# First pair's queries and keys read in fp32 by SyncE's queue and converted on chip, pair 0's bias rows fetched by SyncE's queue: the opening of a fused attention and feed-forward kernel

## The chip, the cores and the metric

The kernel runs on one core of one Trainium2 chip. The metric is the device time of one execution in microseconds (us). Each profile is one such execution, and times inside it count from the span's start. PE is TensorE, ACT ScalarE, DVE VectorE, POOL GpSimd, SP SyncE. All runs used here are of the fast state, except e8's single run, whose state can't be told. Runs of the same kernel still differ by 1.7 us (changed kernel, 17 runs) to 2.9 us (kernel before, 39 runs), which matters for everything below.

## The reference, cut to what matters

```python
# q, k, v: (8, 8, 576, 64) fp32; bias_table: (32, 8)
scores = q @ k.transpose(0, 1, 3, 2) / 8 + bias[bucket]      # relative-position bias per head
attn   = softmax(scores)
x      = (attn @ v)  -> (4608, 512)
out    = ((x @ w_a) * (x @ w_b)) @ w_out                      # bilinear feed-forward
```

Heads are worked on in 32 pairs; "pair 0" is the first two heads of the first batch. The bias is applied after the exponential, as a multiplication by exp(bias), whose rows lie in a small table that the kernel computes and writes to DRAM.

## The kernel before: the parts concerned

Almost all inputs are cast to bf16 on their way by POOL's loads. An "opening" string gives the hand-made order of the first 70 us or so: `<k0` is a load, `TK0`/`TQ0` transposes of pair 0's keys and queries on PE, `CK`/`CQ` copies of them out of PSUM (`:A` on ACT, `:D` on DVE), `S001` a score block (pair, half, key block), `E001` its exponential on ACT, `M001` the multiplication by bias on DVE, `w1` a filler: a multiplication of zeros on PE.

```python
def load4(src, dst, b, h0, h1):                       # casts fp32 -> bf16, POOL
    nc.gpsimd.dma_start(
        out=dst[:, 256 * h0:256 * h1].rearrange("p (h x) -> p h x", x=256),
        in_=src[b, h0:h1, 0:SM, :].rearrange("h (p t) d -> p h (t d)", t=NM))
# ...
nc.sync.dma_start(out=bt_sb[0:NB, :], in_=bias_table)
nc.scalar.dma_start(out=bl_sb[0:NB, :], ...)
nc.sync.dma_start(out=oh_sb[0:NB, :], in_=oh_handle.ap())     # one-hot buckets
nc.scalar.dma_start(out=ident[:, :], in_=id_handle.ap())      # identity for transposes
# ...
warm_up(5)
nc.scalar.activation(out=eb_sb[0:NB, :], in_=bt_sb[0:NB, :], func=ACTF.Exp)
nc.tensor.matmul(out=tps[0:H, 0:NR], lhsT=eb_sb[0:NB, :], rhs=oh_sb[0:NB, :], ...)
warm_up(2)
# ...
nc.sync.dma_start(out=tab.ap(), in_=tab_sb[0:H, :])           # the bias table, to DRAM

def load_w(hp, y0, y1):                               # bias rows of a pair, POOL
    nc.gpsimd.dma_start(out=W_sb[hp][:, :, y0:y1], in_=bass.AP(tensor=tab, ...))
# ...
opening = """
    <k0 <q0 <k1 <q123h0 <k23 <tk <W0 <v0 <W1 <vtb <vta ...
    <wb2 <wo TK0 PC0:A TQ0 PF1:D PX1:D PV1:A PU0:D CK0:A CQ00:A CQ01... w1 S001 ... S000 E001 E000
    w1 TQ30 PC1:D TK1 ... TQ10 CQ10:D S011 E011 ...                      # cut
"""
```

The softmax here doesn't subtract the row's maximum and nothing guards it: scores larger than these inputs give would overflow.

## Time and profile before

| | kernel before |
|---|---|
| median of 3 runs (first measurement) | 414.23 us |
| PE busy | 404.5 of 412.2 us |
| first exponential on ACT | 8.01 us |
| pair 0's keys and queries landed | 4.4 (first used at 4.70) and 6.15 us |
| bias table landed (POOL goes on) | 8.31 us |
| PE at full clock from | 13.9 us |

The timeline of PE around 13.9 us (columns: start, length, engine, line, operation, result and operands, shape, count).

```profile
13.35 0.61 PE L446 MATMUL qkh<-QT,KT 64*128 64x256 bf16 x4
13.88 0.39 PE L237 MATMUL warm<-zero_sb 128*128 128x512 bf16 x1
14.21 0.39 PE L446 MATMUL qkh<-QT,KT 64*128 64x256 bf16 x4
```

The same four score multiplications take 0.61 us ahead of 13.88 us and 0.39 us after it. That is how to read the release of PE's clock from a profile: the clock row of the page shows 9 in all slices and the table of windows 1.00 even before 13.9 us, since the trace's clock record only begins with its first change, here at 13.86 us.

### The profile page before, as it was taken

What the parts mean: (1) busy time and instruction counts of PE and PEld (TensorE: products, weight loads), DVE (VectorE), ACT (ScalarE), POOL (GpSimd) and SP (SyncE); (2) the same over time, 40 slices, a digit from 0 to 9 for tenths busy, and PEclk for the clock granted to TensorE, in tenths of its full rate; (3) what the DMA queues carried; (4) which work ended last, traced back from release to release, by engine and by line L of the source; (5) the groups of instructions that cost most, each with busy time, mean ns of one, the idle gap of its engine ahead of it and who ended that gap; (6) DMA issues with size and microseconds to landing.
All of it is one profiled execution on the core that took longest, in us unless ns stands there. A gap on an engine that the chain in (4) does not pass through costs nothing.

```text
span 412.2 us, 8768 instructions
## 1 busy us (share of the span) xinstructions
PE 404.5 (98%) x3473; PEld 210.0 (51%) x3473; DVE 240.8 (58%) x568; ACT 251.3 (61%) x384; POOL 133.6 (32%) x191
## 2 busy tenths in 40 slices
PE   8999999999999999999999999999999999999996
PEld 3576656455555455455444555555545554444443
DVE  3898997366745665476656764667547652421320
ACT  4998992676748665677556765767486642322321
POOL 6967547788029300960079004300000000000000
PEclk9999999999999999999999999999999999999999
DMA  8999999999979914995299709960520012002004
GB/s 104 179 202 189 206 166 144 160 193 142 87 133 159 139 34 91 155 129 90 41 161 143 116 16 126 127 92 17 117 67 16 17 40 78 0 9 95 2 2 102
DMA packets 135786, 42.05 MB, mean 102 GB/s; under 512 B 113688, under 2 KB 130968, under 8 KB 135744
## 3 DMA queue, kind: packets, MB, share of 16 engines
q0 software_dynamic: 81712, 20.27, 56.3%
q1 hardware_dynamic: 48592, 11.87, 18.6%
q10 hardware_dynamic: 5440, 9.34, 7.2%
q8 instruction: 27, 0.44, 0.5%
q14 instruction: 15, 0.12, 0.1%
HBM read 39.18 MB, written 9.45 MB: 118 GB/s over the span
## 4 chain that ended last, share of the span: by engine, by line
PE 94%; DVE 2%; ACT 2%; DMA 1%; issue 1%; ACTq 0%; POOL 0%; POOLq 0%
PE pb L633 23%; PE pa L633 23%; PE po L670 22%; PE av L569 8%; PE qk L406 7%; PE av L559 2%; PE av L563 2%; PE qkh L446 1%; PE qkt L479 1%; DMA qn<-in_q_dram 1%; PE trb L321 1%; ACT ath L452 1%; PE trb L415 1%; PE trb L609 0%; DVE ath L461 0%
## 5 line engine op out<-in xcount | busy, mean ns | idle before, releaser
L430 ACT ACTIVATE at<-qk 128x1024 bf16<-128x1024 f32 x112 | 113.3, 1028 | 27.5 <-DMA out_dram<-ob 10.3
L643 DVE TENSOR_TENSOR g<-pb,ha 128x512 bf16<-128x512 f32 (+1 forms) x114 | 75.6, 664 | 75.0 <-PE pb L633 58.9
L633 PE MATMUL pb<-xn,wb 128*128 128x512 bf16 (+1 forms) x456 | 112.1, 368 | 0.2 <-DVE g L643 0.2
L633 PE MATMUL pa<-xn,wa 128*128 128x512 bf16 (+1 forms) x456 | 112.1, 368 | 0.0
L640 ACT ACTIVATE ha<-pa 128x512 f32<-128x512 f32 (+1 forms) x114 | 66.2, 581 | 67.7 <-PE pa L633 66.2
L670 PE MATMUL po<-wo,g 128*128 128x512 bf16 x420 | 98.2, 379 | 0.0
L435 DVE TENSOR_TENSOR at<-at,W 128x1024 bf16<-128x1024 bf16 x112 | 75.1, 686 | 22.2 <-ACT at L430 22.1
L633 PEld LDWEIGHTS <-wa 128*128 128x128 bf16 x456 | 41.2, 98 | 46.3 <-issue 6.6
L633 PEld LDWEIGHTS <-wb 128*128 128x128 bf16 x456 | 40.6, 97 | 43.6 <-issue 5.2
L670 PEld LDWEIGHTS <-g 128*128 128x128 bf16 x420 | 38.9, 98 | 44.9 <-issue 2.5
L675 ACT ACTIVATE ob<-po 128x512 f32<-128x512 f32 x34 | 20.4, 600 | 39.9 <-PE po L670 33.6
L569 PE MATMUL av<-vm,at 128*128 128x65 bf16 x896 | 41.2, 193 | 0.0
L569 PEld LDWEIGHTS <-at 128*128 128x128 bf16 x896 | 37.4, 97 | 6.3
L132 POOL DMA_DIRECT2D qn<-in_q_dram x48 | 36.4, 807 | 12.0 <-PE qk L406 6.9
L170 POOL DMA_DIRECT2D vt<-in_v_dram x12 | 7.4, 620 | 98.9 <-PE av L563 98.1
L580 DVE RECIPROCAL rc<-av 128x6 f32<-128x6 f32 (+1 forms) x64 | 11.9, 186 | 45.2 <-PE av L569 40.8
L141 POOL DMA_DIRECT2D kn<-in_k_dram x48 | 36.2, 794 | 1.4 <-issue 0.7
L559 PE MATMUL av<-vt,att 128*128 128x130 bf16 x152 | 33.6, 221 | 0.0
L406 PE MATMUL qk<-QB,KB 64*128 64x512 bf16 x192 | 29.1, 381 | 0.0
L582 DVE TENSOR_TENSOR XG<-av,rc 128x384 bf16<-128x384 f32 (+2 forms) x64 | 27.2, 425 | 2.2
L506 ACT ACTIVATE att<-qkt 128x640 bf16<-128x640 f32 x24 | 16.8, 701 | 13.0 <-PE qkt L480 13.0
L559 PEld LDWEIGHTS <-att 128*128 128x128 bf16 x152 | 15.0, 98 | 6.5
(104 smaller groups left out, 327.0 us busy)
## 6 DMA issues: line engine op xcount, KB each, us to landing
out_dram<-ob ACTq DMA_DIRECT2D x31, 256.0 KB, 3.1
vn<-in_v_dram POOLq DMA_DIRECT2D x16, 256.0 KB, 5.8
kn<-in_k_dram POOLq DMA_DIRECT2D x48, 64.0 KB, 5.0
qn<-in_q_dram POOLq DMA_DIRECT2D x48, 64.0 KB, 4.4
wa<-in_moe_w_a_dram POOLq DMA_DIRECT2D x3, 512.0 KB, 7.4
wb<-in_moe_w_b_dram POOLq DMA_DIRECT2D x3, 512.0 KB, 9.2
wo<-in_moe_w_out_dram POOLq DMA_DIRECT2D x1, 1536.0 KB, 15.6
xn<-XG SPq DMA_TRANSPOSE x52, 3.0
```

The lines of the kernel that those rows point to most:

```text
L132: nc.gpsimd.dma_start(out=by_tile(qn[b % 2])[:, h0 // 4, t, :, :], in_=q[b, h0:h1, 128 * t:128 * t + 128, :].transpose([1, 0, 2]))
L141: nc.gpsimd.dma_start(out=by_tile(kn[b % 2])[:, h0 // 4, t, :, :], in_=k[b, h0:h1, t:SM:NM, :].transpose([1, 0, 2]))
L406: nc.tensor.matmul(out=ps[:, hh, :], lhsT=kT[r, t, :], rhs=qT[r, :, :], start=True, stop=True)
L430: nc.scalar.activation(out=at[:, :, :], in_=ps[:, :, :], func=ACTF.Exp, scale=scale)
L435: nc.vector.tensor_tensor(out=at[:, :, :], in0=at[:, :, :], in1=w[:, :, S - 1 + t:S - 1 + t - SM:-1], op=MULT)
L559: nc.tensor.matmul(out=pav[:, slot, :, :], lhsT=weights_tail(p, jq), rhs=vt[i][:, :, hp, :], start=True, stop=True)
L569: nc.tensor.matmul(out=pav[:, slot, hh, :], lhsT=weights(p, t, hh, jq), rhs=vm[i][:, 2 * hp + hh, t, :], start=False, stop=True, skip_grou ...
L582: nc.vector.tensor_tensor(out=xg[:, jqs[0]:jqs[0] + m, :, :], in0=pav[:, 0:m, :, 0:Dh], in1=rc[:, 0:m, :].unsqueeze(3).to_broadcast([128, ...
L633: nc.tensor.matmul(out=ps[:, 0:n], lhsT=w[df // 4][:, mc, 128 * (df % 4):128 * (df % 4) + 128], rhs=xn_sb[mc][:, 512 * c + lo:512 * c + lo ...
L640: nc.scalar.activation(out=ha[:, 0:n], in_=ff["pa", df, lo][:, 0:n], func=ACTF.Copy)
L643: nc.vector.tensor_tensor(out=g_sb[df][:, lo:lo + n], in0=ff["pb", df, lo][:, 0:n], in1=ff["ha", df, lo][:, 0:n], op=MULT)
L670: nc.tensor.matmul(out=po[:, :], lhsT=g_sb[df][:, 128 * tt:128 * tt + 128], rhs=wo_sb[:, df, :], start=(df == 0), stop=(df == NDF - 1))
```

## The change

Its intent: SyncE's queue is idle at the start while POOL's list of casting loads is long. So pair 0's queries and keys are read as fp32 by SyncE and converted by ACT and DVE, POOL starts with other loads, and pair 0's bias rows also go to SyncE, right behind the table's store. The two constants become one load, and the opening is put in a new order.

```diff
-    nc.sync.dma_start(out=bt_sb[0:NB, :], in_=bias_table)
+    def load_first(x, dst):
+        nc.sync.dma_start(out=dst.rearrange("p (h x) -> p h x", x=256),
+                          in_=x[0, 0:2, 0:SM, :].rearrange("h (p t) d -> p h (t d)", t=NM))
+    nc.sync.dma_start(out=cn_sb[:, :], in_=cn_handle.ap())     # identity and one-hot, joined
+    load_first(q, kq32[1])
+    load_first(k, kq32[0])
+    nc.scalar.dma_start(out=bt_sb[0:NB, :], in_=bias_table)
 ...
-            load_w(int(name[1]), *(...))
+            load_w(int(name[1]), *(...), nc.sync if name in ('W0',) else nc.gpsimd)
 ...
-        <k0 <q0 <k1 <q123h0 <k23 <tk <W0 <v0 <W1 <vtb <vta <tq <W2 <R0 ...
-        <wb2 <wo TK0 PC0:A TQ0 ... w1 S001 PX0:D CQ01:A S000 E001 E000
-        w1 TQ30 PC1:D TK1 CK1:D TQ10 CQ10:D S011 E011 ...
+        <q123h0 <k1 <tk <vtb <k23 <W1 <W0 <v0 <vta <tq <W2 <W3 ...
+        PC0:A PX0:D YQ0:A PC1:A PU0:D PV0:A PX1:D TQ0 YK0:D TK0 CQ00:A CQ01:D CK0:D TQ10 PF1:A CQ10:D
+        S000 E000 PV1:D S001 E001 TK1 CK1:D TQ30 TZ1 CZ1:D S011 ...
 ...
+        elif kind == "YK":
+            copy(eng, kn[0][:, 0:512], kq32[0])                 # fp32 -> bf16
+        elif kind == "YQ":
+            copy(eng, qn[0][:, 0:512], kq32[1])
```

More of the change, by code (lines that the diff above doesn't have):

```diff
@@ L73 @@
     oh_np[bucket, np.arange(NR)] = 1.0
-    oh_handle = nc.inline_tensor(oh_np.astype(ml_dtypes.bfloat16), name="oh_const")
-    id_handle = nc.inline_tensor(np.eye(128).astype(ml_dtypes.bfloat16), name="id_const")
-    oh_sb = const.tile([128, NR], BF16, name="oh_sb")
-    ident = const.tile([128, 128], BF16, name="ident")
+    cn_np = np.zeros((128, NR + 128), dtype=np.float32)
+    cn_np[0:NB, 0:NR] = oh_np
+    cn_np[:, NR:] = np.eye(128)
+    cn_handle = nc.inline_tensor(cn_np.astype(ml_dtypes.bfloat16), name="cn_const")
+    cn_sb = const.tile([128, NR + 128], BF16, name="cn_sb")
+    oh_sb = cn_sb[:, 0:NR]
+    ident = cn_sb[:, NR:NR + 128]
     bt_sb = const.tile([128, H], FP32, name="bt_sb")
@@ L114 @@
     ob_last = wpool.tile([128, DM], FP32, name="ob_last")
+    kq32 = [xn_sb[i][:, NT - 1024:NT].bitcast(FP32) for i in range(2)]
     g_sb = [wpool.tile([128, DM], BF16, name=f"g{df}") for df in range(NDF)]
@@ L224 @@
                                     ap=[[0, NB], [1, H]]))
-    nc.sync.dma_start(out=oh_sb[0:NB, :], in_=oh_handle.ap())
-    nc.scalar.dma_start(out=ident[:, :], in_=id_handle.ap())
     nc.vector.memset(zero_sb[:, :], 0.0)
@@ L249, with load_w @@
     nc.vector.tensor_copy(out=tab_sb[0:H, c0:c0 + NR], in_=tps[0:H, 0:NR])
-    def load_w(hp, y0, y1):
-        nc.gpsimd.dma_start(out=W_sb[hp][:, :, y0:y1],
+    def load_w(hp, y0, y1, eng):
+        eng.dma_start(out=W_sb[hp][:, :, y0:y1],
                           in_=bass.AP(tensor=tab, offset=2 * hp * TB + y0,
@@ L295, in load @@
         elif name[0] in "WR":
-            load_w(int(name[1]), *((320, NY) if name[0] == "W" else (0, 320)))
+            load_w(int(name[1]), *((320, NY) if name[0] == "W" else (0, 320)), nc.sync if name in ('W0',) else nc.gpsimd)
         else:
@@ L728 @@
     opening = """
-        <k0 <q0 <k1 <q123h0 <k23 <tk <W0 <v0 <W1 <vtb <vta <tq <W2 <R0 <v1 <Wta <q123h1 <W3 <Wtb <R1
-        <wa0 <k4 <wb0 <R2 <R3 <q4 <k5 <uq <q7 <q5 <wa1 <wb1 <k6 <uk <vt1b <k7 <vb1a <vb1b <vt1a <wa2 <q6
-        <wb2 <wo TK0 PC0:A TQ0 PF1:D PX1:D PV1:A PU0:D CK0:A CQ00:D w1 S001 PX0:D CQ01:A S000 E001 E000
-        w1 TQ30 PC1:D TK1 CK1:D TQ10 CQ10:D S011 E011 CQ30:D TK3 S100 E100 TZ1 CK3:D S301 M001 TQ20
-        PV0:D TK2 E301 S101 E101 CQ20:D CK2:D w1 S200 E200 CZ1:D M000 w1 KS w1 S201 EK w2 S010 E201 V0:D
@@ L734 @@
-        M101 TZ0 M100 M200 M201 AV00 N00 CZ0:A AV10 E010 X00 CX00:A S300 E300 N10 T0 V1:D X10 CX10:A
-        M010 ET0 AV20 TQ11 TQ21 M011 N20 CQ11:A S110 S111 CQ21:A E110 X20 M301 TQ31 M300 AV30 T1 PW:D
-        MT0 AV01 CX20:D M110 E111 N30 ET1 X30 M111 CQ31:A T2 ET2 S210 CX30:D E210 PF0:A LH FA0a N01 HA0a
-        MT1 TK4 X01 T3 AV11 ET3 CX01:D S211 PU1:D FB0a FA1a E211 CK4:D HA1a N11 X11 G0a M210 S310 MT2
-        CX11:A E310 FB1a G1a S311 FA2a HA2a TQ4 M211 CQ4:A FB2a AV21 E311 FA3a HA3a TQ5 MT3 M310 S43 S42
@@ L739 @@
-        CQ5:A G2a FB3a N21 M311 TK5 E43 E42 TZ0x G3a CZ0x:D AV31 LV CK5:D N31 FA4a HA4a X21 TQ7 CQ7:A
-        S41 E41 S52 E52 CX21:D FB4a FA5a HA5a X31 G4a TK6 M43 FB5a CX31:D S40 E40 S53 G5a FA0b FB0b
-        CK6:D M41 TZ1x HA0b G0b CZ1x:D S51 FA1b FB1b E53 M53 HA1b G1b E51 TK7 CK7:D M40 FA2b HA2b S50
-        E50 FB2b FA3b G2b HA3b V2:D T4 FB3b FA4b V3:D ET4 G3b S70 E70 M42 MT4 M52 HA4b FB4b G4b TQ6 T5
-        ET5 M50 CQ6:A AV40 N40 MT5 M51 FA5b S71 E71 HA5b S73 FB5b AV41 G5b M70 N41 S72 E73 FA6f E72 T6
@@ L744 @@
-        M73 M71 HA6f FB6f G6f AV50 N50 S62 ET6 MT6 E62 S61 FA7f HA7f M62 AV51 N51 TH S60 E61 M61 FB7f
-        G7f E60 M60 S63 E63 M63 FA8f HA8f M72 T7 FB8f G8f AV60 N60 ET7 MT7 FA9f HA9f FB9f G9f AV70 FA10f
-        FB10f N70 HA10f G10f AV71 FA11f N71 FB11f X71 HA11f G11f AV61 N61 X70 FO00 FO01 FO02 HO0 CX70:D
-        CX71:D
+        <q123h0 <k1 <tk <vtb <k23 <W1 <W0 <v0 <vta <tq <W2 <W3 <v1 <Wta <q123h1 <R0 <Wtb <R1 <k4 <wa0
+        <wb0 <R2 <uq <q5 <q4 <R3 <k5 <wa1 <q7 <wb1 <k6 <uk <k7 <vb1a <vb1b <vt1a <q6 <wb2 <vt1b <wa2 <wo
@@ new lines @@
+        PC0:A PX0:D YQ0:A PC1:A PU0:D PV0:A PX1:D TQ0 YK0:D TK0 CQ00:A CQ01:D CK0:D TQ10 PF1:A CQ10:D
+        S000 E000 PV1:D S001 E001 TK1 CK1:D TQ30 TZ1 CZ1:D S011 CQ30:D E011 S101 TQ20 CQ20:D E101 M101
+        S100 E100 TK3 CK3:D KS EK M000 TK2 S301 E301 CK2:D w2 S200 E200 M100 M001 w1 S201 E201 V0:D
+        PU1:D w2 S300 E300 M200 M201 AV00 TZ0 AV10 S010 CZ0:A N00 T0 N10 E010 X10 X00 CX00:A V1:D AV20
+        CX10:A TQ11 TQ21 M301 M300 ET0 AV30 CQ11:A S110 CQ21:A N20 M010 M011 PW:A MT0 S111 TQ31 E110 X20
@@ new lines @@
+        CQ31:A E111 T1 ET1 N30 M110 X30 CX20:D CX30:D AV01 T2 TK4 M111 S210 ET2 E210 FA0a HA0a N01 T3
+        MT1 X01 AV11 CK4:D CX01:A PF0:D LH ET3 N11 S211 E211 FB0a FA1a HA1a X11 G0a MT2 CX11:D S310 E310
+        FB1a G1a S311 M210 FA2a FB2a HA2a E311 TQ5 TQ4 CQ4:A M211 FA3a AV21 CQ5:A S42 G2a S43 FB3a TZ0x
+        MT3 M311 HA3a M310 TK5 E42 N21 FA4a HA4a CZ0x:D AV31 LV CK5:D X21 E43 TQ7 CQ7:A G3a N31 S41 E41
+        S52 E52 FB4a FA5a HA5a CX21:D G4a M43 TK6 X31 CX31:D FB5a S40 E40 CK6:D S53 G5a FA0b HA0b TZ1x
@@ new lines @@
+        M41 CZ1x:D FB0b G0b S51 E53 FA1b HA1b TK7 FB1b FA2b E51 M52 HA2b CK7:D S50 G1b V2:D FB2b FA3b
+        E50 V3:D G2b HA3b T4 M40 FB3b G3b S70 M42 ET4 MT4 FA4b FB4b T5 HA4b M53 E70 G4b TQ6 ET5 M51
+        CQ6:A AV40 N40 FA5b S71 E71 S73 MT5 M50 FB5b HA5b AV41 S72 E73 G5b N41 M71 FA6f M73 T6 E72 M72
+        ET6 MT6 AV50 FB6f HA6f N50 S62 S61 E62 G6f M62 FA7f HA7f AV51 N51 TH S60 E61 M61 FB7f G7f E60
+        M60 S63 E63 FA8f HA8f T7 ET7 M63 M70 FB8f G8f AV60 FA9f FB9f N60 MT7 AV70 HA9f G9f FA10f HA10f
@@ L748 @@
+        FB10f N70 AV71 G10f FA11f HA11f FB11f N71 X71 AV61 X70 FO00 G11f N61 FO01 FO02 CX71:D CX70:D HO0
     """
```

## The prediction

> **What bounds the kernel now.** I read the page first: its busy line and its slices say which engine and which stretch matter.
>
> ```profile
> PE 404.5 (98%) x3473; PEld 210.0 (51%) x3473; DVE 240.8 (58%) x568; ACT 251.3 (61%) x384; POOL 133.6 (32%) x191
> ...
> PE   8999999999999999999999999999999999999996
> ...
> DMA  8999999999979914995299709960520012002004
> ```
>
> PE is busy for 404.5 of 412.2 us. Of the 7.7 us that are left, 4.1 lie in the last slice (windows 400 to 412.2: 8.13 of 12.20 us busy), where the last output drains. The diff doesn't touch that end: its order of late instructions is the same. So the change can only act at the start. The windows of the first 24 us give PE 2.00 minus 0.81, 2.00 minus 1.34, and gaps of 0.2 to 0.5 us later on: about 3.6 us idle, of which 1.19 us come before anything can run.
>
> Idle time alone is not the measure, because that stretch holds fillers (multiplications of zeros) that count as busy. I therefore read the chain of waits for the first 25 us (columns: start, length, what).
>
> ```profile
> 2.06 4.09 DMA qn<-in_q_dram
> 6.16 0.04 issue
> 6.20 0.64 PE trb L321 x8
> ...
> 13.99 1.94 ACT ath L452 x2
> 15.93 0.51 ACT atk L471
> ...
> 21.86 0.41 ACT QT L311
> 22.27 0.04 issue
> 22.31 0.61 PE qkh L446 x8
> ```
>
> It begins with one DMA: pair 0's queries, issued by POOL at 2.06 us, land at about 6.15. From 22.31 to 405.5 us nearly every piece is PE, and the waits of PE after 26 us add up to 0.2 us. So the time is: when PE's unbroken run begins, plus the work left in it, plus a fixed end. What matters is what holds PE before 22 us. The timeline of ACT says it.
>
> ```profile
> 7.34 0.38 ACT L311 ACTIVATE QT<-trb 128x256 bf16<-128x256 bf16 x1 [1.33 <-DVE QT L313]
> 8.01 1.94 ACT L452 ACTIVATE ath<-qkh 128x1024 bf16<-128x1024 f32 x2 [0.28 <-PE qkh L446]
> 10.79 3.05 ACT L452 ACTIVATE ath<-qkh 128x1024 bf16<-128x1024 f32 x3 [0.84 <-PE qkh L446]
> 13.99 1.94 ACT L452 ACTIVATE ath<-qkh 128x1024 bf16<-128x1024 f32 x2 [0.16 <-PE qkh L446]
> ```
>
> The first exponential starts at 8.01 us. From then to 21.86 ACT is full apart from holes of 0.84 and 0.16 us: 11 exponentials of 1024 columns at about 1.0 us, one of 896 at 0.92, and small copies. **In the opening ACT's chain of exponentials is the bound**, and its start is set by the landing of the queries. DVE is close behind: 1.5 to 2.0 us in each 2 us window from 14 us.
>
> Last, the timeline of POOL and SyncE's queue.
>
> ```profile
> 4.29 0.31 SPq L257 DMA_DIRECT2D bias_tab<-wo  x1
> ...
> 4.91 0.74 POOL L158 DMA_DIRECT2D tlc<-in_k_dram  x1
> ...
> 8.31 0.72 POOL L252 DMA_DIRECT2D W<-bias_tab  x1 [2.66 <-DMA bias_tab<-wo]
> ```
>
> POOL issues one load per 0.72 to 0.8 us, and stands still 2.66 us until the bias table, written to DRAM at 4.29, has landed near 8.3. Everything behind it in POOL's order waits too.
>
> **What the Trainium skill says.** "DMA: Bandwidth & Descriptors", section "SWDGE vs HWDGE vs iDMA", says that a DMA that casts can only be issued from GpSimd, a plain one also from SyncE or ScalarE. This explains why the move needs fp32 landing tiles and conversions; in the trace all loads that become bf16 are indeed POOL's. Its "Specifications" put the first-byte latency near 1 us by GpSimd and 0.6 us by SyncE; the trace has 1.7 us from issue to landing for SyncE's small loads against 3.1 us at best for POOL's keys, which is the same direction, though those move more. Its section "Issuing engines are not separate DMA queues" says that all of them run on the same 16 engines and only issue time is saved; the trace is consistent, with DMA at 9 tenths in the next slices whoever issues. "TensorE: Matmul & The Clock Gate", Part 1, says that PE starts at half clock and is released by sustained activity: here eight 64x256 multiplications take 1.04 us at 7.36 and 0.61 us at 22.31, and fillers fall from 0.61 to 0.39 us at 13.88, so this trace shows one release near 13.9 us.
>
> **The change part by part.**
>
> 1. Pair 0's queries and keys leave POOL's list (0.82 + 0.74 us of issue) and go to SyncE's queue, behind one constant load (identity and one-hot table joined, 128 x 384 bf16 = 98 KB). SyncE starts at 0.74 us and needs 0.41 per issue: constants 0.74, q 1.2, k 1.65. Bytes: q and k are 128 x 512 x 4 = 262 KB each, in 1 KB pieces. As a rough rate I take the 147 to 160 GB/s of the finer DMA slices from 3 to 5 us; those count bf16, and fp32 was read for it, so I allow twice, about 300 GB/s for fp32. Constants and q, 360 KB, are then 1.2 us of transfer, k another 0.9. With 1.7 us of fixed time from 0.74 and POOL's first loads sharing the engines, I get q landed at 4.0 to 4.6, k at 4.9 to 5.6 us (before: k 4.70, q 6.15). The later of the two comes 0.6 to 1.2 us sooner.
> 2. Added: two conversions of 128x512. On ACT 0.60 us, from the copy of KT of that size. On DVE about 0.5 us, an estimate from its 256-column f32 fill at 0.27. Only k's lies on the path; q's is done by about 5 us, when ACT is idle anyway. Cost on the path: 0.5 us.
> 3. From there as before: eight transposes 0.64, a copy 0.42, four multiplications 0.5 us; before, 6.16 to 8.01 = 1.85 us. The changed kernel's instruction order puts pair 1's first query transposes between keys and scores, but they run during the copy. So the first exponential starts at 4.9..5.6 + 0.5 + 1.85 = 7.25 to 7.95: **0.1 to 0.75 us sooner** than 8.01, say 0.5.
> 4. POOL's other early loads move up by two places. Pair 1..3's queries go from 3.49 to 1.25, pair 1's keys from 2.77 to about 2.0. The 0.84 us hole came from the third score block, which stood behind pair 3's and 1's transposes; now pair 0's and 1's are ready sooner. I count 0.5 of the 0.84 + 0.16 us as won.
> 5. Pair 0's bias rows go to SyncE, right behind the table's store. One POOL issue of 0.73 us less; W1 takes the place of W0 after the wait. But the bias difference now needs the second ACT load (1.22 + 1.8 = 3.0 instead of 2.54 us), so the table is some 0.4 us later, and its store stands in SyncE's queue behind 0.5 MB of q and k. I expect its landing at 8.3 to 9.2 us.
> 6. The opening order is rearranged, and two fillers go. Pair 3's first output block now precedes the scores that began the unbroken run (1.0 us of PE work earlier), but PE can only use that if ACT and DVE keep up. ACT gains the copy of the bias tails (about 0.4 us), DVE loses it.
>
> Sum: 0.5 (start) + 0.5 (hole) + up to 0.6 (order, fillers, an issue fewer) = 1.6 us, minus about 0.4 for the later table and ACT's extra copy: **1.2 us of 414.2**, so 413.0.
>
> **Rivals.**
>
> - *The bias table becomes the wait.* DVE's first multiplication by bias now needs W1, which POOL can issue only when the table has landed. In the changed order a copy of pair 3's keys stands behind it on DVE, and scores behind that. For: the store lies behind the big loads, and W took at least 3.1 us to land, so 8.7 + 3.1 = 11.8 or later, where DVE's first such multiplication was at 11.69. Against: nothing waited for W in the trace before. It would eat most of the gain: 413.8 to 414.8.
> - *The DMA engines are shared, so nothing lands sooner.* For: slices at 9. Against: the first 2 us have a DMA share of 0.02, free time for SyncE's early issue. It would make k land near 6 us and the time 414.
> - *The gain is taken back at the first weights.* They are issued at 17.9 and 19.4 and take 7.4 and 9.3 us, so the second lands near 28.7, only 0.8 us before its first use at 29.51; POOL's count of issues before them hardly changes. For a shift over 0.8 us PE would wait there: 413.4.
> - *The clock is released a window later*, as early fillers are gone: up to 1 us lost, 414.2. For: nearly all early work is small and transposes. Against: ACT, not PE, is the bound there.
>
> **Range and chances.** My sum says 413.0, the rivals mostly cost 0.4 to 1.5 us, and better overlap of the new order could give another 1 us: 411.9 to 414.4. The runs before spread 0.7 us. Two per cent are 8.3 us; the whole idle time of PE is 7.7 us with 4.1 of it untouched, so faster by 2% is as good as excluded, and slower would need several new waits at once: 0.01 each.
>
> **What would show it.** Right: queries landed by 4.6 us and keys by 5.6, first 1024-column exponential at 7.2 to 7.9 us, no hole over 0.4 us behind the second, table landed by 9 us, PE unbroken from about 21 us, end unchanged. Wrong: first exponential at 8 us or later (sharing), DVE waiting for W near 12 us (table), PE waiting for a weight load at 25 to 29 us (weights), fillers or scores at 0.6 us per 512 columns after 14 us (clock).

## The result, and the profile after

In the first comparison, six runs of each, the changed kernel had a median of 413.23 us (412.73 to 413.90) against 414.43 us (413.61 to 415.46). The ratio is 0.997, 95% interval 0.9953 to 0.9987. Ratios here are the mean time of one kernel's fast runs over the mean of the other's of the same rounds, so not quite the ratio of the medians.

The profiled run of the changed kernel happens to be its slowest (413.90 us, span 412.1 us), and lies level with the profile of before (span 412.2 us). So this pair of traces shows the mechanism, not the 1.2 us. First the chain of waits at the start (start, length, what).

```profile
1.72 4.51 DMA xn<-in_k_dram
6.25 0.44 DVE kn L322
6.69 0.04 issue
6.73 0.68 PE trk L330 x8
7.43 0.44 DVE KT L322
7.87 0.05 issue
7.92 1.03 PE qkh L455 x8
```

The chain again begins with one DMA, now SyncE's load of the keys (`xn` is their fp32 landing place). It takes 4.51 us, and what waits for it starts at 6.25 us, 0.05 us after what waited for the queries before (6.20 us). And what waits is now a conversion of 0.44 us that was not there. The scores start at 7.92 us instead of 7.36. Next, ACT's timeline.

```profile
8.57 1.94 ACT L461 ACTIVATE ath<-qkh 128x1024 bf16<-128x1024 f32 x2 [1.97 <-PE qkh L455]
10.67 2.86 ACT L461 ACTIVATE ath<-qkh 128x1024 bf16<-128x1024 f32 x3 [0.17 <-PE qkh L455]
13.93 1.02 ACT L480 ACTIVATE atk<-qkt 128x1024 bf16<-128x1024 f32 x1 [0.40 <-PE qkt L476]
15.04 1.02 ACT L461 ACTIVATE ath<-qkh 128x1024 bf16<-128x1024 f32 x1
16.55 2.95 ACT L461 ACTIVATE ath<-qkh 128x1024 bf16<-128x1024 f32 x3 [0.48 <-PE qkh L455]
```

The first exponential is at 8.57 us, 0.56 us later than before. The hole of 0.84 us behind the second has shrunk to 0.17, but holes of 0.40 and 0.48 us follow. PE's timeline shows what stands ahead of the last of these.

```profile
15.33 0.63 PE L246 MATMUL warm<-zero_sb 128*128 128x512 bf16 x1 [0.33 <-issue]
15.90 0.61 PE L455 MATMUL qkh<-QT,KT 64*128 64x256 bf16 x4
...
16.98 0.54 PE L455 MATMUL qkh<-QT,KT 64*128 64x256 bf16 x4
...
17.98 0.39 PE L455 MATMUL qkh<-QT,KT 64*128 64x256 bf16 x4
```

The score block that ACT waits for, from 16.06 to 16.55 us, stands behind a filler, and both still run at half pace. The four multiplications come down to 0.39 us only behind 17 us: the trace's clock record puts the release at 17.31 us, 3.45 us later than before. The timeline of all engines has SyncE's queue, POOL's next load and DVE's first multiplication by bias:

```profile
4.48 0.35 SPq L266 DMA_DIRECT2D bias_tab<-wo  x1
...
7.80 0.39 SPq L261 DMA_DIRECT2D W<-bias_tab  x1
8.07 0.72 POOL L261 DMA_DIRECT2D W<-bias_tab  x1 [3.24 <-DMA bias_tab<-wo]
...
12.64 0.69 DVE L470 TENSOR_TENSOR ath<-ath,W 128x1024 bf16<-128x1024 bf16 x1 [0.44 <-ACT ath L461]
```

The table has landed by 7.8 us, sooner than the 8.31 of before, and DVE's first multiplication waits for ACT, not for bias rows. Last, the DMA queues between 4 and 5 us (queue 0 is POOL's, queue 1 SyncE's; shares of the 16 engines' time, which can overlap).

```profile
q0 software_dynamic: 199, 0.10, 74.2%
q1 hardware_dynamic: 133, 0.14, 49.8%
```

Both queues are at work at once, in the very time in which the keys are awaited.

To compare progress further on, I counted PE's weight loads from the end of the program, which is the same in both kernels behind the opening. The start of the one that is 3100 from the end, called **PE's mark** below, is at 32.80 us before and 33.21 us in the changed kernel. (The two orders stand at different instructions there, so a mark compares exactly only within one order.) From there the distance between two profiles changes little (0.38 us at loads 2500 and 1500), so what the opening decides is decided by 33 us.

At the last load, though, the distance is 0.05 us. The other 0.33 us are won in one place far behind the opening (first before, then the changed kernel):

```profile
224.36 1.02 PE L633 MATMUL pb<-xn,wb 128*128 128x512 bf16 x4 [0.17 <-DVE g L643]
224.41 1.03 PE L642 MATMUL pb<-xn,wb 128*128 128x512 bf16 x4
```

Before, PE waits there for DVE, and two weight loads are 0.39 us apart that are 0.06 us apart in the changed kernel. Both profiles of the old program (before and e6 below) have this wait, all twelve of the changed program and its variants lack it, e3 with the old order too. Why is not shown; no run looks at it.

### The profile page after: what moved, and what is told of

The parts are those of the page before. It is cut to its first block, busy times and chain, and to the rows that moved or that the text cites. A ratio compares the mean times of both kernels' runs of the same rounds, so it can differ in the third digit from the quotient of the medians.

```text
span 412.1 us, 8718 instructions
## 1 busy us (share of the span) xinstructions
PE 401.5 (97%) x3420; PEld 209.6 (51%) x3471; DVE 240.6 (58%) x568; ACT 252.0 (61%) x386; POOL 131.4 (32%) x188
## 4 chain that ended last, share of the span: by engine, by line
PE 95%; DMA 1%; ACT 1%; issue 1%; DVE 0%; ACTq 0%; SPq 0%
PE pb L642 23%; PE pa L642 23%; PE po L679 22%; PE av L578 8%; PE qk L415 7%; PE av L568 2%; PE av L572 2%; PE qkh L455 1%; PE qkt L488 1%; DMA xn<-in_k_dram 1%; PE trb L330 1%; PE trb L424 1%; PE trk L330 1%; ACT ath L461 0%; PE qkt L494 0%
## 5 line engine op out<-in xcount | busy, mean ns | idle before, releaser
L642 PE MATMUL pa<-xn,wa 128*128 128x512 bf16 (+1 forms) x440 | 110.8, 368 | 0.7
L679 PE MATMUL po<-wo,g 128*128 128x512 bf16 x403 | 95.5, 379 | 0.8
```

Of the source, the lines that this page charges most:

```text
L642: nc.tensor.matmul(out=ps[:, 0:n], lhsT=w[df // 4][:, mc, 128 * (df % 4):128 * (df % 4) + 128], rhs=xn_sb[mc][:, 512 * c + lo:512 * c + lo ...
L679: nc.tensor.matmul(out=po[:, :], lhsT=g_sb[df][:, 128 * tt:128 * tt + 128], rhs=wo_sb[:, df, :], start=(df == 0), stop=(df == NDF - 1))
```

## The experiments

All gave correct results on the chip. Summary, with the time of the first 1024-column exponential, the release of the clock that PE then keeps, and PE's mark, each from the run's one profile. Ratios are to the kernel before on the same chip.

| run | median, us | lowest to highest | ratio (95%) | first exp. | release | mark |
|---|---|---|---|---|---|---|
| before | 414.01 (39 runs) | 412.60 to 415.46 | | 8.01 | 13.86 | 32.80 |
| changed, first measurement | 413.23 | 412.73 to 413.90 | 0.997 (0.9953 to 0.9987) | 8.57 | 17.31 | 33.21 |
| e1, changed again | 414.11 | 413.72 to 414.41 | 1.0004 (0.9984 to 1.0024) | 8.63 | 17.67 | 33.36 |
| e9, changed a third time | 413.86 | 413.71 to 414.41 | 1.0003 (0.9991 to 1.0015) | 8.78 | 18.29 | 33.75 |
| e2, bf16 loads | 413.87 | 413.19 to 414.12 | 0.9997 (0.9978 to 1.0016) | 8.42 | 16.48 | 32.93 |
| e3, old order | 414.37 | 414.00 to 414.87 | 1.0011 (0.9992 to 1.0030) | 9.07 | 15.86 | 33.80 |
| e4, early fillers | 413.81 | 411.61 to 414.55 | 0.999 (0.9964 to 1.0016) | 9.25 | 17.04 | 33.89 |
| e5, dense fillers | 412.79 | 412.48 to 413.98 | 0.997 (0.9951 to 0.9989) | 8.31 | 14.64 | 32.14 |
| e6, dense fillers, kernel before | 414.76 | 413.39 to 415.82 | 1.0006 (0.9983 to 1.0028) | 7.40 | 5.31 | 34.63 |
| e7, bf16 loads, scores first | 413.68 | 413.33 to 414.71 | 0.999 (0.9972 to 1.0008) | 7.77 | 16.31 | 32.56 |
| e8, POOL held (one look) | 412.95 | | | 7.53 | 16.01 | 32.28 |
| e10, bias rows by POOL | 414.23 | 413.94 to 414.52 | 1.0009 (0.9997 to 1.0021) | 8.93 | 18.20 | 33.79 |
| e11, POOL held, timed | 413.63 | 412.16 to 414.81 | 0.999 (0.9972 to 1.0009) | 7.98 | 17.41 | 33.51 |
| e12, POOL held and a filler | 413.19 | 411.89 to 413.75 | 0.998 (0.9965 to 0.9995) | 8.24 | 14.80 | 32.25 |

### e1 and e9: the changed kernel again

No edit; asked was whether 1.2 us repeats, and what varies from run to run.

> The changed kernel once more, to see what its runs and its trace vary in. Its first profiled run (413.90 us, the slowest of six) showed keys landing at 6.25 us, first exponential at 8.57 us and the release of PE's clock only near 17 us, where the kernel before had 8.01 us and 13.9 us. Theory 'clock by chance': the release varies from run to run by some 3 us and explains most of the 1.2 us between runs; then this profile shows another release time and a span that follows it by about half the shift. Theory 'order of work': the release is where the instructions put it, and this profile repeats 17 us and 412 us of span. Both: median 413.0 to 413.5, keys again near 6.2 us because the DMA engines are shared.

> The changed kernel a third time, on the chip of the three runs that follow, as their measure. On the first chip it was 0.997 of the kernel before, on the second 1.0004. Theory 'the change is worth 1.2 us': 0.997 again. Theory 'it is worth 0 to 0.5 us and the rest is which step of 3.4 us the clock is released in': between 0.998 and 1.001, keys landed at 6.2 to 6.3 us, first exponential at 8.5 to 8.7 us.

It did not repeat: ratios 1.0004 and 1.0003 in two later sessions. All 17 runs of the changed kernel together have a median of 413.85 us, all 39 of the kernel before 414.01 us. The keys again landed at 6.30 and 6.69 us. The first of e1's theories, that the release wanders by some 3 us in the changed kernel, is not what the final releases show (17.31, 17.67, 18.29 us), but e9 shows something else, in the table of windows (busy time of PE, PEld, DVE, ACT, POOL, then the clock, DMA share and GB/s):

```profile
4.60:8.00 3.40, 1.32 (x25) 0.71 (x24) 1.50 (x7) 1.75 (x5) 0.23 (x1) 1.00 1.55 210
8.00:18.20 10.20, 9.57 (x84) 4.36 (x85) 6.79 (x17) 8.22 (x9) 9.66 (x14) 0.50 1.07 162
```

Here the clock was released early, at 4.64 us, taken back at 8.05 us after a stretch in which PE was busy for only 1.32 of 3.40 us, and given again at 18.29 us. The steps are multiples of one length: 3.41 and 10.24 us. This run's mean clock is 0.985. Two of the six runs of the first measurement have 0.992, which would fit two such steps at half clock (2 x 3.41 x 0.5 / 412 = 0.008), and are its fastest (412.73 and 412.75 us); no profile of them was kept, so this is an inference. The record speaks against a low mean clock as the cause of a fast run: seven runs of the kernel before with 0.988 to 0.991 took 413.82 to 415.46 us, and e5's slowest (413.98 us) has 0.992. Without the two runs the other four still average 413.46 us, so they don't explain the whole 1.2 us.

### e2: pair 0 by POOL's casting loads again, the rest of the change kept

```diff
-    load_first(q, kq32[1])
-    load_first(k, kq32[0])
-        <q123h0 <k1 <tk ... YQ0:A ... YK0:D
+        <k0 <q0 <q123h0 <k1 <tk ...
```

> The changed kernel with pair 0's queries and keys again cast by POOL's loads, first in its list, and no conversions; everything else of the change kept. Theory 'the plain path of the loads is the gain': 414.2 or more. Theory 'the new order and the bias rows on SyncE are the gain': 413.0 to 413.6, since keys landed no sooner by SyncE (6.25 us) than queries did by POOL (6.15 us). Against the second: POOL has two issues more ahead of all else (1.5 us), which could move pair 1's keys and the bias rows later and cost 0.5 us.

The same time as the changed kernel on that chip, 0.24 us lower in the median, which is within the spread. Without the part that gives the change its name nothing is lost. The line that held the scores back:

```profile
7.42 0.42 PE L337 MATMUL trb<-cn_sb,qn 64*64 64x64 bf16 x8 [1.12 <-DMA qn<-in_q_dram]
```

Pair 1's query transposes stand ahead of pair 0's scores in PE's order and waited 1.12 us for their load, now third in POOL's list.

### e3: the new loads with the old order of work

```diff
-        (new order)
+        <k1 <q123h0 <k23 <tk <W0 ... YQ0:A TQ0 PC0:A ... YK0:D TK0 PV1:A CK0:A ... (rest as before)
```

> The loads of the change (pair 0's queries and keys in fp32 by SyncE with conversions, bias rows of pair 0 by SyncE, joined constants) with the order of the opening work as in the kernel before, only that pair 0's queries are transposed ahead of its keys. Theory 'loads': 413.2, all of the gain. Theory 'new order': 414.2 or worse, since the first score block waits for keys at 6.25 us plus a conversion where it had 6.15 us without one. The old order has fillers in PE's early waits, so the clock should be released near 13.9 us again.

The loads alone gain nothing: 414.37 us, and the first exponential is at 9.07 us. This is the slowest of the four of its call, by 0.26 us against e1, within the noise of six runs; its mark (33.80 us) is 0.44 us behind e1's.

### e4, e5, e6: fillers to bring the clock's release forward

e4 adds four fillers in PE's early waits; e5 replaces the two rows of fillers of the changed kernel, e6 those of the kernel before.

```diff
 # e4:  TQ0 w2 YK0:D TK0 ...  CK0:D TQ10 w1 ... S001 E001 w1 TK1
-    warm_up(5)   # e5 and e6: 6
-    warm_up(2)   # e5: 5, e6: 4
```

> The changed kernel with four fillers more, of 512 columns each, in PE's early waits (two behind the first transposes, where PE idles 1.0 us for the keys, one ahead of the first scores, one behind them). Theory 'late release of the clock costs': release comes a window earlier (near 13.9 us or sooner) and the median falls by 0.3 to 1.0 us below the changed kernel's. Theory 'ACT is the bound there': release may come sooner, the time stays within 0.2 us or grows by the fillers that stand in the way (up to 0.5 us).

> The changed kernel with PE kept full of fillers from 1.2 to about 6.1 us (6 and 5 of them in place of 5 and 2), which is the time in which it waits for the keys anyway (6.25 us in its profiles). In the four profiles of the changed order the clock was released at 15.9 to 17.7 us, in the kernel before at 13.9. Theory 'a late release costs': the release comes by 7 us or one step of 3.4 us later, and the median falls by 0.5 to 2 us against the changed kernel (best single run of the version with four fillers: 411.61). Theory 'ACT is the bound, the clock costs nothing': release sooner, time within 0.3 us.

> The kernel before with the same: fillers (6 and 4) until the transposes of the keys at about 5.6 us, which the first scores don't wait for, as the queries land at 6.15. Theory 'a late release costs': the median falls by 0.3 to 1.5 us below the kernel before; the gap between this and the version above is then the change's own worth without the clock's luck, and I expect it within 0.5 us of zero, since both kernels' profiles put PE at the same work within 0.4 us. Theory 'the clock costs nothing': same as before within 0.3 us.

e4's profile shows no earlier release (17.04 us), but two of its runs were at 411.61 and 412.74 us while three stayed above 414.3: undecided. **e5 has the lowest median of all**: its trace has the clock at full from 4.40 to 11.22 us, at half for one step, and at full from 14.64 us. Its median is 412.79 us, the ratio 0.997 with an interval clear of 1. ACT's timeline shows where the profiled run gained:

```profile
8.31 4.69 ACT L461 ACTIVATE ath<-qkh 128x1024 bf16<-128x1024 f32 x5 [1.52 <-PE qkh L455]
13.40 1.02 ACT L480 ACTIVATE atk<-qkt 128x1024 bf16<-128x1024 f32 x1 [0.40 <-PE qkt L476]
14.51 3.81 ACT L461 ACTIVATE ath<-qkh 128x1024 bf16<-128x1024 f32 x4
```

The keys landed no sooner (6.43 us), yet five exponentials follow without a hole and later four, where the changed kernel had holes of 0.17 and 0.48 us. PE's mark is 1.07 us ahead. That is one profile; and the ratio of 0.997 is the one that the changed kernel's first measurement had and its repeats did not. e5 was timed once, and the changed kernel was not timed beside it, so its gain still needs a repeat.

e6 failed in an instructive way. The clock was at full from 5.31 us on and the first exponential at 7.40 us, the earliest of all, and still the kernel was not faster. From DVE's timeline:

```profile
12.44 0.70 DVE L461 TENSOR_TENSOR ath<-ath,W 128x1024 bf16<-128x1024 bf16 x1 [1.51 <-DMA W<-bias_tab]
```

and from the table of waits (who waited for what, and the longest waits in us):

```profile
PE pb L633 <- DMA wb<-in_moe_w_b_dram: 1.4, 1, 1.4
```

The sixth filler delayed the table's multiplication by 0.42 us (3.86 instead of 3.44 us), the table landed at 9.37 us, DVE waited for bias rows, all of POOL's list moved back 1.1 to 1.5 us, and PE waited 1.4 us for weights. The expected gap of at most 0.5 us between e5 and e6 was wrong: it is 1.97 us in the medians. So e6 doesn't tell what the clock is worth in the old order; it shows that the old order has the bias rows and the weights close behind. The changed order had a table almost as late in e5 (9.02 us), and DVE waited for bias rows there too:

```profile
12.38 0.70 DVE L470 TENSOR_TENSOR ath<-ath,W 128x1024 bf16<-128x1024 bf16 x1 [0.98 <-DMA W<-bias_tab]
```

But none of PE's multiplications waited for weights (the weight loads did, by at most 0.3 us), and e5's mark is still the earliest.

### e7: scores ahead of pair 1's query transposes, on e2

```diff
-... CK0:D TQ10 PF1:A CQ10:D S000 E000 PV1:D S001 E001 TK1
+... CK0:D PF1:A S000 E000 PV1:D S001 E001 TQ10 CQ10:D TK1
```

> The version whose pair 0 is again cast by POOL's loads, with pair 1's first query transposes moved behind pair 0's two score blocks (they held PE 1.12 us for a load in its profile). First exponential expected at 7.3 us instead of 8.42. Theory 'the first exponential sets the opening': PE reaches the work at 3100 weight loads from its end 0.6 to 1.1 us sooner than that version (32.93 us), median 413.0 or less. Theory 'what follows (bias rows, pair 1, clock) sets it': the lead is lost by 20 us, same time within 0.3 us.

The first exponential came 0.65 us sooner than in e2 (7.77 us, not the 7.3 expected, since PE waited 0.84 us for the copy of the keys), and PE's mark 0.37 us sooner; a hole of 0.54 us behind the second exponential took the rest. The two runs are on different chips, and each interval reaches 1: inconclusive in time, half of the lead kept in the profile.

### e8 and e11: POOL held back

```diff
+    for _ in range(4):
+        nc.gpsimd.memset(ob_last[:, :], 0.0)      # 2.27 us of POOL, ahead of its first load
 ...  and TQ10 behind the first scores, as in e7
```

> The changed kernel with POOL held back by four fills of 128x512 at the start, so that SyncE's two fp32 loads have the DMA engines to themselves; pair 1's first query transposes stand behind the first scores so that they don't hide it. Theory 'shared engines': keys land 0.8 to 1.5 us sooner than 6.25 us, queries a little sooner than 4.4 us. Theory 'fixed time of the queue or its order': keys land at 6.0 us or later as before. The whole time may grow, as all of POOL's list is late; it is not what this run is for.

> The version with POOL held for 2.3 us and pair 1's query transposes behind the first scores, now timed. In its single look keys were landed by 5.1 us, the first exponential was at 7.53 us and the run at 412.95. Theory 'keys that land a microsecond sooner end the kernel a microsecond sooner': median 0.7 to 1.2 us below the changed kernel's of the same chip. Theory 'luck of the clock': within 0.3 us of it.

The issue-to-landing times of SyncE's two fp32 loads, first of the changed kernel:

```profile
DMA to landing us min/median/max: 3.2/3.9/4.5
```

and of e8:

```profile
DMA to landing us min/median/max: 3.1/3.1/3.2
```

The first number is the queries', the last the keys'. Without POOL's loads beside them the keys land in 3.2 instead of 4.5 us, so at 4.9 us (1.72 + 3.2) instead of 6.25. Issue, queue and the order in it are the same; only POOL's loads are later. **This shows that sharing with POOL's loads cost the keys 1.3 us, the lead that the change was to win.** e11 and e12 repeat it (3.2 and 3.1 us).

How much of it reaches the first exponential varies: 7.53 us in e8, 7.98 in e11 and 8.24 in e12, against 8.01 in the kernel before. The keys' conversion no longer waits for the keys there, but for DVE's earlier work, which hangs on a 1 KB load of the bias table. e8's line, then e11's:

```profile
3.10 0.15 DVE L242 TENSOR_TENSOR bt_sb<-bt_sb,bl_sb 32x8 f32<-32x8 f32 x1 [0.59 <-DMA bl_sb<-in_bias_table_dram]
3.65 0.15 DVE L242 TENSOR_TENSOR bt_sb<-bt_sb,bl_sb 32x8 f32<-32x8 f32 x1 [1.14 <-DMA bl_sb<-in_bias_table_dram]
```

From there DVE's order runs on without a wait for the keys to the conversion, at 5.11 us in e8 and 5.65 us in e11 (5.54 in e12). So part of the 1.3 us is lost again behind the bias table's own chain, which the change also made later.

Timed (e11), the gain against e9 on the same chip is 0.5 us in the means (413.46 and 413.97) and 0.23 in the medians, less than the 0.7 to 1.2 expected, and the intervals overlap. e8 and e11 are one kernel in two profiles: release 16.01 and 17.41 us, table landed by 7.42 and 8.84, mark 32.28 and 33.51, spans 411.2 and 412.4 us. So the opening of an unchanged program wanders by 1.2 us, as much as the first measurement's gain; the bias load that lands 0.55 us later is the earliest difference in DVE's timeline. e11's two fastest runs (412.16 and 412.39) again have a mean clock of 0.992, which elsewhere went with slow runs too (see e9).

### e10: pair 0's bias rows by POOL

```diff
-... nc.sync if name in ('W0',) else nc.gpsimd)        # and <W1 <W0
+... nc.gpsimd)                                        # and <W0 <W1
```

> The changed kernel with pair 0's bias rows fetched by POOL again, first behind its wait for the table; everything else kept. All of POOL's later list is one issue (0.73 us) later. Theory 'this half of the change matters': 0.3 to 0.7 us slower than the changed kernel of the same chip, with DVE waiting for bias rows near 12 us or PE for weights near 28 us. Theory 'it is hidden': within 0.2 us, which six runs that spread over 1 us cannot tell; then PE's place at 3100 weight loads from the end (33.2 to 33.4 us in the changed kernel) decides.

0.27 us slower than e9 in the means, which doesn't exceed the spread; the marks are level (33.79 and 33.75 us), and neither of the two waits showed. In the profile this half of the change is hidden.

### e12: POOL held, one filler more

```diff
 # e11 and:
-    warm_up(2)
+    warm_up(3)
```

> The same with one filler more (5 and 3) between the table's multiplication and the first transposes, so that PE has no rest from 1.2 to 6.2 us but 0.2 us. Theory 'a release before 8 us is worth 1 us': where the profile shows it, PE is at 3100 weight loads from the end by 31.5 us instead of 32.3, and the median is 412.0 to 412.5, best of all. If the one filler doesn't bring the release forward: as the version above.

The profile shows no release before 8 us, but one at 14.80 us in place of 17.41; the mark is 32.25 us although the first exponential, at 8.24 us, was later than in e11. The median is 413.19 us, the ratio 0.998 with an interval just below 1. In this one call it beats the kernel before, and e9 by 0.96 us in the means. e5 has the lowest median of all, but was timed on another chip, so which of the two is better is open.

## Why the prediction was right or wrong

**The numbers.** 413.0 us, 411.9 to 414.4 and "within 2%" all hold for the first measurement. But two repeats put the changed kernel level with the one before, so the 1.2 us forecast are not shown to be the change's worth. That number was met partly by chance. Over all runs I would put it between 0 and 0.6 us, an estimate: the means of all runs are 414.07 and 413.74 us, 0.33 us apart. In the profiles 0.33 us are won at 224 us and none in the opening, where the changed kernel is behind. Why the first measurement showed more is open.

**Step 1, landing: this is the step that failed.** It said "k at 4.9 to 5.6 us". Measured: 6.25 to 6.69 us in three profiles of the changed kernel. The term "POOL's first loads sharing the engines" was in the text but mis-sized. Without it the text's own sum is 4.5 us (0.74 + 1.7 + 1.2 + 0.9), so the range allowed 0.4 to 1.1 us for it. With POOL held the keys landed at 4.9 us, and beside POOL's loads 1.3 us (first profile) to 1.7 us (e9) later. The queries' 4.0 to 4.6 us was right (4.39). The "before: k 4.70" is the time at which PE first used the keys; they had landed near 4.4 us (1.25 + 3.1), which changes nothing, as the queries came last.

**Step 2, conversions: right.** 0.63 us on ACT and 0.43 on DVE against 0.60 and about 0.5.

**Step 3, first exponential: wrong by step 1.** "7.25 to 7.95" was 8.57 to 8.78 us, later than before instead of 0.5 us sooner. From the keys' landing on, the working was right: 6.25 + 0.44 + 1.85 = 8.54.

**Step 4, the hole: right and given back.** 0.84 us became 0.17. The new holes of 0.40 and 0.48 us were not foreseen, and with them the holes add up to 1.05 us, where they were 1.00 (0.84 + 0.16); e5 shows that the second of them and the 0.17 go when the clock is released sooner, the 0.40 doesn't.

**Step 5, the table: not later.** The bias difference did come later (3.18 us, before 2.59), but the store was issued only 0.19 us later (4.48), and the table landed by 7.8 to 8.3 us in the changed kernel's profiles, at or below the expected 8.3 to 9.2. The 0.4 us taken off the sum for it and for ACT's extra copy were thus too many.

**Step 6, order: not settled.** e3 is the slowest of its call, which fits a small gain from the order with these loads, within noise. That the new order bears a late table better is suggested by e5 against e6, one profile of each.

**Rivals.** "Nothing lands sooner" came true; its 414 us fits the repeats better than my sum. "The clock is released a window later" came true as well in the profiles (17.31 for 13.86 us; of the kernel before there is only one), and the argument against it, that ACT is the bound, was too simple: score blocks and fillers at half pace open holes in ACT's chain. Bias rows and weights did not become waits in the changed kernel's three profiles. Bias rows did in e5 (0.98 us), e6 (1.51) and e8 (0.9), weights in e6 (1.4). Over the eleven profiles of the changed order and its variants, a fit gives a mark 0.5 us later per us of a later first exponential and 0.4 us later per us of a later release, to within 0.4 us. That is a fit to profiles in which both moved, not a measurement of either alone.

**The bounds and the end: right but for 0.33 us.** The last outputs drain the same, and no window past 60 us gained or lost over 0.4 us. But "the change can only act at the start" missed the wait at 224 us.

## What to carry to other kernels

Moving a load to an idle queue bought issue time here, not bandwidth: look at what the other queues transfer in the same microseconds, hold back what is not needed yet, and then look for the next wait behind it. In the profiles, fillers that keep PE busy early (e5, mark 32.14 us) were worth as much as keys that land 1.3 us sooner (e8 and e11, 32.28 and 33.51 us), but not where the path to the next wait stood behind them (e6). And where an unchanged kernel's profiles differ by 1 us, a gain of 1 us needs a repeat in another session before it is believed.

## What the Trainium skill lacked or had wrong

- "TensorE: Matmul & The Clock Gate", Part 1, names the busy window (about 3.4 us, agreed: steps of 3.41, 6.83 and 10.24 us here) but gives no share of it that must be busy for a release, nor one below which the clock is taken back. In the changed kernel PE was busy for 8.81 of the 9.30 us from 8.00 to 17.30 us, and the release came only at 17.31 us; e9 lost the full clock after a stretch with 1.32 of 3.40 us busy.
- "DMA: Bandwidth & Descriptors", "Issuing engines are not separate DMA queues", says that transfers of several queues interleave, which agrees, but gives no size: 262 KB of keys took 4.5 us beside POOL's loads and 3.2 us without them.
- No page says that the clock shown by a profile can be that of an unrecorded start: windows ahead of the first change showed 1.00 while four 64x256 multiplications took 0.61 us, against 0.39 us at the full clock.
